# One fp32 block chain on one core: w3·w_out in the order of the tiles' conversion, output operands two units ahead, low parts on VectorE, output weights loaded further ahead

## The chip, the core and the metric

One core of a Trainium2 chip. The metric is the device time of the whole program in microseconds (us); less is better. Times shown are medians of several executions, and a profile is one further execution with the hardware profiler.

## What is computed

Attention with a bias of cumulative gates, then a feed-forward block with g = h - tanh(h), then a gated block whose two inner products are multiplied; all in fp32.

```python
x = attention(q, k, v, s)            # 2304 tokens x 512
h = x @ w_in; x = (h - tanh(h)) @ w_out
a = x @ w1;  b = x @ w2              # 2304 x 1024 each
h = a * b @ w3                       # 1024 x 1024
return h @ w_out2                    # 1024 x 512
```

## The kernel before

Every fp32 matrix is split into a high part, the value cast to the matmul's short fp32 type (ScalarE, line 64), and a low part, the rest (line 65: `lo`, on GpSimd if the caller names no other). A product is three matmuls: high*high, high*low, low*high (`mm3`, line 113).

There are three phases. The first, to about 425 us, is attention, mixed with half of the feed-forward block. The second (`ffn_rest`) is the other half; beside it `preparations` (line 654) brings the weights of the last block into shape: w1 and w2 into seven sums and differences for each of eight column groups (DRAM tensor `wg_d`), and w3 into `w3_d`, eight tiles f = 0 to 7 of 1 MB, high and low part. A tile is converted into a `park` buffer, of which there are two, and stored (line 683).

The third phase has two steps. First, w3 @ w_out2 is worked out (lines 820 to 837), so that the last two products become one. For each f the tile is loaded from `w3_d` into a `park` buffer (`w3b`, line 823), 24 matmuls make `w3o`, and ScalarE copies it to a ring tile `wf` (line 831). `weights` makes from each four of these one half h of the seven output weights (`wkA`, `wkS`), which line 817 stores to `wo_d`, 512 KB each; the first half's are made in this loop, the second's in the first seven units. In the loop also stand the loads of the weights S and A of units 0 and 1 (`load_unit`, behind tiles 2 and 4), and `need(0)`, which makes one operand of the first token block at each step.

Second, the two products with w1 and w2, the multiplication, and the product with the combined weight run over three blocks `sb` of 768 tokens, as seven-product schemes (Strassen-Winograd: T1 to T4 are sums and differences of the operand quarters B11 to B22, S1 to S4 those of the weights). A unit u is a block and a column group f, 24 in all. It has seven groups of six matmuls of 384 columns, in the order A11 (bank W), A12 (V), S2 (W), S4 (Y), S3 (W), then S1 of the next unit (Y, `first_y`), A22 (W). Between them ScalarE copies (s1, u2, s5) and VectorE adds (c11 from V, c12 from Y, c22 from W) take the partial sums out; Y has one bank, so the next unit's Y waits for c12, and A22 waits for c22. Two multiplications (lines 966 and 967, the second on GpSimd) give a quarter of the next product's operand.

The combined weight's product for block sb (`class Out`) is done in the units of block sb + 1: at f = 0 to 6 two bursts of 12 matmuls, `burst(f, 0)` behind A12 and `burst(f, 1)` behind S4. A burst needs `operand(f)`, made at the end of the unit before: for T1 to T4 two subtractions (tso, line 885), and for all two casts on ScalarE and two low parts on VectorE, into one of two ring buffers. It needs the weight `load(f)`, issued one unit ahead into four half buffers `wo`. At the last block nothing follows, and the seven products run as a tail of 24 matmuls each (lines 981 to 987).

At the change of block, `operands(sb + 1)` makes seven operands of the next block; in it GpSimd makes the low parts of B11, B21 and B22, and VectorE those of T1 to T4 (line 769).

DMAs are issued by SyncE's queue (SP) alone. A planner orders the instructions of each engine by a simulated timeline, and may move them ahead of their place in the program; on TensorE it keeps program order where `manual_schedule` has been entered, in the kernel before from line 841 on, so behind the w3 loop. An engine runs its queue in order.

Of the kernel before, what the change touches and what calls it, by code (L numbers as in the profile page):

```python
# [15 lines left out]
P = 128  # L16
# [3 lines left out]
DM = 512  # L20
# [17 lines left out]
def tile_kernel(ctx: ExitStack, tc: tile.TileContext, qk, v, s, w_in, w_out, w1, w2, w3t, w_o2, outT):  # L38
# [24 lines left out]
    def split(dst_hi, dst_lo, src, hi=None, lo=None):  # L63
        i = (hi or nc.scalar.copy)(dst_hi, src)  # L64
        (lo or nc.gpsimd.tensor_sub)(dst_lo, src, dst_hi.bitcast(F32))  # L65
        return i
# [584 lines left out]
    def load_w3(f, z):  # L651
        return load_raw(w3t[f, :, 4 * z:4 * z + 4].rearrange("p m c -> p (m c)"), f"w3_{f}_{z}", behind=pace[0])

    def preparations():

        for f in range(NG):
            a = plain(load_raw(w1[f], f"w1_{f}", behind=pace[0]), f"w1_{f}")
            yield
            b = plain(load_raw(w2[f], f"w2_{f}", behind=pace[0]), f"w2_{f}")
            a11, a12, a21, a22 = a[:, :2 * P], a[:, 2 * P:], b[:, :2 * P], b[:, 2 * P:]  # L660
            cs = b2.tile([P, 4, 2 * P], F32, tag="cs", name=f"cs{f}", bufs=1)
            for z, (x, y, fn) in enumerate(((a21, a22, nc.vector.tensor_add), (cs[:, 0], a11, nc.vector.tensor_sub),
                                            (a11, a21, nc.vector.tensor_sub), (a12, cs[:, 1], nc.vector.tensor_sub))):
                fn(cs[:, z], x, y)
            pk = wt.tile([P, 4, 2, 2 * P], F32R, tag="park", name=f"pka{f}", bufs=2)
            for z, x in ((0, a[:, :].rearrange("p (z c) -> p z c", z=2)), (2, a22.unsqueeze(1))):
                n = x.shape[1]
                split(pk[:, z:z + n, 0], pk[:, z:z + n, 1], x, lo=nc.vector.tensor_sub)
            nc.sync.dma_start(wg_d[f, :, 4:], pk[:, :3].bitcast(F32))
            pk = wt.tile([P, 4, 2, 2 * P], F32R, tag="park", name=f"pks{f}", bufs=2)  # L670
            split(pk[:, :, 0], pk[:, :, 1], cs, lo=nc.vector.tensor_sub)
            nc.sync.dma_start(wg_d[f, :, :4], pk.bitcast(F32))
            yield
        for f in range(NG):
            if f == NG // 2:
                for m in range(NG):
                    convert(load_raw(w_o2[m], f"wo2_{m}", behind=pace[0]), f"wo2_{m}", wo2[m], lo=nc.vector.tensor_sub)
                    yield
            pk = wt.tile([P, 2, 2, DM], F32R, tag="park", name=f"w3p{f}", bufs=2)
            for z in range(2):  # L680
                convert(load_w3(f, z), f"w3_{f}_{z}", pk[:, z], lo=nc.vector.tensor_sub)
                yield
            nc.sync.dma_start(w3_d[f], pk.bitcast(F32))

    with ExitStack() as bctx:
        b2 = bctx.enter_context(tc.tile_pool(name="b2", bufs=2, reuse_waits="tile"))
# [67 lines left out]
    def operands(sb):  # L754

        c0 = 2 * T * sb
        b11, b12, b21, b22 = (xy[:, c:c + 2, c0 + T * t:c0 + T * t + T] for c in (0, 2) for t in (0, 1))
        full = {"B11": b11, "B21": b21, "B22": b22}
        out = {}
        for o in OPS:  # L760
            if o in full:
                x = full[o]
            else:
                x = r3.tile([P, 2, T], F32, tag="ts", name=f"{o}_{sb}", bufs=2)
                full[o] = x
                a, b = {"T1": (b12, b11), "T2": (b22, full["T1"]), "T3": (b22, b12), "T4": (b21, full.get("T2"))}[o]
                nc.vector.tensor_sub(x, a, b)
            w = r3.tile([P, 2, 2, T], F32R, tag="tb", name=f"{o}hl_{sb}", bufs=8)
            split(w[:, 0], w[:, 1], x, lo=nc.vector.tensor_sub if o[0] == "T" else None)
            out[o] = w  # L770
            yield out

# [4 lines left out]
    def load_unit(u):  # L777
        if u >= len(units):
            return
        f = units[u][1]  # L780
        ws = r3.tile([P, 4, 2, 2 * P], F32R, tag="ws", name=f"S_{u}", bufs=2)
        nc.sync.dma_start(ws.bitcast(F32), wg_d[f, :, :4])
        wa = r3.tile([P, 3, 2, 2 * P], F32R, tag="wa", name=f"A_{u}", bufs=2)
        nc.sync.dma_start(wa.bitcast(F32), wg_d[f, :, 4:])
        wts[u] = {o: ws[:, n] if n < 4 else wa[:, n - 4] for o, n in WOP.items()}
# [13 lines left out]
    def ring(name):  # L799
        return r3.tile([P, 6, DM], F32, tag="ring", name=name, bufs=2)  # L800
# [17 lines left out]
            yield  # L818

    wf, made, last = [], [], {}  # L820
    for f in range(NG):
        w3 = wt.tile([P, 2, 2, DM], F32R, tag="park", name=f"w3b{f}", bufs=2)
        nc.sync.dma_start(w3.bitcast(F32), w3_d[f])
        if f in (2, 4):
            load_unit(f // 2 - 1)
        ps = ps3.tile([P, 512], F32, tag=f"o{f % 2}", name=f"w3o{f}")
        for m in range(NG):
            mm3(ps, w3[:, m // 4], P * (m % 4), wo2[m][:, 0, :], wo2[m][:, 1, :], m == 0, m == NG - 1)
        if f % 4 == 0:
            wf.append(ring(f"wf{f // 4}"))  # L830
        nc.scalar.copy(wf[-1][:, f % 4], ps)
        if f % 4 == 3:
            made.append(weights(f // 4, wf[-1]))
        if f >= NG // 2:
            for _ in range(2):
                next(made[0], None)
        need(0)

    lctx.close()
    l3 = ctx.enter_context(tc.tile_pool(name="l3", bufs=2, reuse_waits="tile"))  # L840
    ctx.enter_context(tc.manual_schedule(engines={mybir.EngineType.PE}))

    def temp(name, u, dt=F32):
        return l3.tile([P, T], dt, tag=name, name=f"{name}_{u}")
# [18 lines left out]
    class Out:  # L863
# [25 lines left out]

        def load(self, n):  # L890
            self.ws[n] = []
            for h in range(2):
                k = r3.tile([P, 2, 2, 2 * P], F32R, tag="wo", name=f"wo{n}_{h}_{self.sb}", bufs=4)
                after_pe(nc.sync.dma_start(k.bitcast(F32), wo_d[n, h]), last.get("pe"))
                self.ws[n].append(k)

# [30 lines left out]
    for u, (sb, f) in enumerate(units):  # L927
# [7 lines left out]
        last["pe"] = group(w, wu["A11"], b["B11"], True, False)  # L935
        if old and f < 6:
            old.load(f + 1)
        if f == NG - 1:
            new.load(0)
        s1 = temp("s1", u)  # L940
        nc.scalar.copy(s1, w[:, :T])
        vv = bank("V", f"V_{u}")
        group(vv, wu["A12"], b["B21"], True, True)
        c11 = temp("c11", u)
        nc.vector.tensor_add(c11, vv[:, :T], s1)
        if old and f < 7:
            old.burst(f, 0)
        group(w, wu["S2"], b["T2"], False, False)
        u2 = temp("u2", u)
# [2 lines left out]
        c12 = temp("c12", u)  # L952
        nc.vector.tensor_add(c12, y[:, :T], u2)
        if old and f < 7:
            old.burst(f, 1)
        group(w, wu["S3"], b["T3"], False, False)
        c22 = temp("c22", u)
        last["c22"] = nc.vector.tensor_add(c22, w[:, :T], s5)  # L958
        if nxt:
            y, s5 = first_y(u + 1)  # L960
        group(w, wu["A22"], b["T4"], False, True)
        if nxt and f == NG - 1:
            for _ in OPS[1:]:
# [3 lines left out]
        (nc.gpsimd if nxt else nc.vector).tensor_mul(new.b[d2][:, f // 2], c12, c22)  # L967
        if sb == 0:
            next(made[1], None)
        if old and f < 6:  # L970
            old.operand(f + 1)
        if f == 6:
            if u < len(units) - 2:
                got = operands(sb + 1)
# [4 lines left out]
            new.operand(0 if nxt else 1)  # L979
    last.clear()  # L980
    for n in range(7):
        if n < 6:
            new.load(n + 1)
        for j in range(2):
            new.burst(n, j)
        if n < 5:
            new.operand(n + 2)
# [39 lines left out]
```

## Time and profile before

| | us |
|---|---|
| runs, median (all three) | 954.67 (949.22, 954.67, 955.17) |
| profiled execution | 953.33 |
| its span, first to last instruction | 951.5 |
| TensorE matmuls busy | 921.0 |
| VectorE busy | 646.5 |
| ScalarE busy | 452.2 |
| GpSimd busy | 231.0 |

The profile names engines PE (TensorE's matmuls), PEld (its weight loads), DVE (VectorE), ACT (ScalarE), POOL (GpSimd) and SP (SyncE); "SPq" is an instruction by which SP issues a DMA. L65 is line 65. A tile's name has its buffer numbers left out: `w3b<-w_d` is the load of a w3 tile, `oY<-T1o,wo` a burst. Matmuls are pipelined: one's start-to-start distance is less than its duration. The granted clock is a share of TensorE's full 2.4 GHz; its other level is 1.2 GHz.

### The profile page before, as it was taken

To read this page: it belongs to the slowest core of one execution; us is meant where nothing else is said; L and a number is where in the kernel's file an instruction comes from. 1 tells how busy PE (TensorE), PEld (TensorE's weight loads), DVE (VectorE), ACT (ScalarE), POOL (GpSimd) and SP (SyncE) were. 2 spreads that over 40 slices of the span, in tenths; PEclk is the share of its full clock that TensorE was granted. 3 is DMA by queue.
4 is the path that set the end of the run, shared out by engine and by line. 5 is a ranking of instruction groups with operands and counts; after the bars stand their busy time and mean duration, and the time that the engine had idled before them with its cause. 6 is when DMAs were issued, how large, how long until landed. Compare 5 with 4: busy or idle time off the path is not lost.

```text
span 951.5 us, 16425 instructions
## 1 busy us (share of the span) xinstructions
PE 921.0 (97%) x6022; PEld 803.0 (84%) x6025; DVE 646.5 (68%) x1394; ACT 452.2 (48%) x1061; POOL 231.0 (24%) x219
## 2 busy tenths in 40 slices
PE   8889999899999999999999999998999999999998
PEld 4467778788888889998888888986899999999997
DVE  7677767687787866767999887673145546744654
ACT  4457877777777743324544343332124232433233
POOL 2245756556565410000000000020024111311100
PEclk9799999999999999999999999999999999999999
DMA  5555365435444523499788644668399767776746
GB/s 161 192 160 171 112 199 189 170 126 183 147 167 145 179 91 98 147 355 362 265 287 302 215 146 177 220 268 295 118 323 332 285 238 288 269 268 234 274 174 218
DMA packets 59648, 203.41 MB, mean 214 GB/s; under 512 B 6608, under 2 KB 21104, under 8 KB 53424
## 3 DMA queue, kind: packets, MB, share of 16 engines
q1 hardware_dynamic: 59568, 202.37, 61.2%
q8 instruction: 47, 0.77, 0.3%
q14 instruction: 33, 0.27, 0.1%
HBM read 153.95 MB, written 48.39 MB: 213 GB/s over the span
## 4 chain that ended last, share of the span: by engine, by line
PE 77%; DVE 9%; DMA 6%; issue 3%; ACT 3%; POOL 1%; SPq 1%; ACTq 0%; DVEq 0%; POOLq 0%
PE yb L117 10%; PE hb L117 10%; PE h L117 8%; PE W L849 8%; PE y L431 7%; PE oW L906 5%; PE w3o L117 4%; PE s_B L229 4%; PE Y L849 4%; PE pv L327 4%; PE oY L906 4%; PE pt_B L301 3%; DVE tso L885 2%; DMA cb<-cum_d 1%; PE V L849 1%
## 5 line engine op out<-in xcount | busy, mean ns | idle before, releaser
L117 PE MATMUL h<-xhl,win 128*128 128x256 f32 x864 | 121.2, 286 | 2.7 <-DVE xhl L65 2.2
L117 PEld LDWEIGHTS h<-xhl,win 128*128 128x128 f32 x864 | 106.2, 188 | 13.7 <-issue 3.9
L117 PE MATMUL hb<-x,win 128*128 128x512 f32 (+1 forms) x480 | 104.9, 367 | 0.0
L117 PEld LDWEIGHTS hb<-x,win 128*128 128x128 f32 x480 | 83.9, 188 | 15.0
L117 PE MATMUL yb<-ghb,wout 128*128 128x512 f32 (+1 forms) x320 | 95.6, 367 | 0.0
L206 POOL TENSOR_SCALAR pr<-cb,cq 128x384 f32<-128x384 f32 (+1 forms) x48 | 89.1, 1869 | 25.0 <-DMA cb<-cum_d 15.2
L431 PE MATMUL y<-gh,wout 128*128 128x256 f32 x576 | 85.5, 288 | 0.0
L290 ACT ACTIVATE pr<-pr,nm 128x128 f32<-128x128 f32 (+2 forms) x120 | 71.5, 598 | 18.6 <-DVE nm L268 18.4
L431 PEld LDWEIGHTS y<-gh,wout 128*128 128x128 f32 x576 | 72.8, 189 | 3.0 <-issue 2.0
L65 POOL TENSOR_TENSOR B11hl<-xy,B11hl 128x768 fp32r<-128x768 f32 x3 | 5.8, 1931 | 276.8 <-ACT B11hl L64 276.8
L117 PEld LDWEIGHTS yb<-ghb,wout 128*128 128x128 f32 x320 | 58.2, 188 | 9.9
L117 PE MATMUL yb<-glb,wout 128*128 128x512 f32 (+1 forms) x160 | 58.4, 367 | 0.0
L301 PE MATMUL pt_B<-ident,pr 96*128 96x96 f32 (+1 forms) x384 | 52.3, 260 | 1.9 <-DVE xy L364 1.0
L967 POOL TENSOR_TENSOR xy<-c,c 128x384 f32<-128x384 f32 x12 | 15.3, 1278 | 148.7 <-DVE c L958 148.7
L117 PE MATMUL w3o<-wo,w3b 128*128 128x512 f32 x192 | 46.0, 400 | 3.9 <-DMA w3b<-w_d 3.9
L268 DVE CUSTOM_DVE_ANT_0 pr<-s_B,pr 96x512 f32<-96x512 f32 (+1 forms) x72 | 44.2, 638 | 8.0 <-PE s_B L229 7.8
L431 PE MATMUL y<-gl,wout 128*128 128x256 f32 x288 | 45.4, 280 | 3.8 <-POOL gl L65 3.8
L117 PEld LDWEIGHTS w3o<-wo,w3b 128*128 128x128 f32 x192 | 36.9, 194 | 12.4 <-issue 4.6
L301 PEld LDWEIGHTS pt_B<-ident,pr 96*128 96x128 f32 (+1 forms) x384 | 41.9, 144 | 6.3 <-issue 3.4
L310 ACT COPY pf_B<-pt_B 128x512 f32<-128x512 f32 (+2 forms) x72 | 35.8, 499 | 22.7 <-PE pt_B L301 22.7
L463 DVE TENSOR_TENSOR th<-h,th 128x256 f32<-128x256 f32 x72 | 30.0, 417 | 22.5 <-ACT th L460 21.7
L460 ACT ACTIVATE th<-h 128x256 f32<-128x256 f32 x72 | 26.9, 374 | 35.3 <-PE h L117 35.3
(213 smaller groups left out, 2093.6 us busy)
## 6 DMA issues: line engine op xcount, KB each, us to landing
S<-wg_d SPq DMA_DIRECT2D x24, 1024.0 KB
wo<-wo_d SPq DMA_DIRECT2D x42, 512.0 KB
A<-wg_d SPq DMA_DIRECT2D x24, 768.0 KB
qk<-in_qk SPq DMA_DIRECT2D x16, 576.0 KB
raw_win<-in_w_in SPq DMA_DIRECT2D x16, 512.0 KB
raw_wout<-in_w_out SPq DMA_DIRECT2D x16, 512.0 KB
raw_w<-in_w SPq DMA_DIRECT2D x16, 512.0 KB
wg_d<-pks SPq DMA_DIRECT2D x8, 1024.0 KB
```

The lines of the kernel that those rows point to most:

```text
L117: i = nc.tensor.matmul(ps, a, b, start=first and n == 0, stop=last and n == 2, skip_group_check=skip)
L206: nc.gpsimd.tensor_scalar(out=t[:pw, e, :w], in0=p.cb[:pw, e, :w], scalar1=c, scalar2=0.0, op0=ALU.add, op1=ALU.min)
L229: latest[0] = nc.tensor.matmul(ps[e][:PW[i], o:o + k1 - k0], w[r, 0, CH0[i]:CH0[i] + PW[i]], x[r, 1, k0:k1], start=z == 0 and (not p.first ...
L268: least[0] = nc.vector.tensor_tensor_reduce(out=t[:pw, k0:k1], in0=ps[:pw, o:o + k1 - k0], in1=t[:pw, k0:k1], scale=-0.125, scalar=nm[:pw, ...
L290: last_exp[0] = nc.scalar.activation(t[:pw, :], t[:pw, :], AF.Exp, bias=m, scale=-1.0, accum_out=p.sums[:pw, e, c:c + 1])
L301: nc.tensor.transpose(pt[:, at:at + pw], p.pr[i][:pw, e, KC0[kj]:KC0[kj] + P], ident[:pw, :pw])
L310: (nc.vector.tensor_copy if j == "B2" and not p.first else nc.scalar.copy)(pf[:, :at], pt[:, :at])
L327: nc.tensor.matmul(p.pv[D * e:D * e + D, c:p.nq], p.vs[:, e, kj], pf[:, beg:end], start=z == 0, stop=z == len(todo) - 1, skip_group_check= ...
L431: nc.tensor.matmul(o, wout[f][:, z, P * c:P * c + P], x, start=f == 0 and n == 0 and c % 2 == 0, stop=f == F1 - 1 and n == 2, skip_group_c ...
L463: nc.vector.tensor_sub(t, hh, t)
L849: i = nc.tensor.matmul(ps[:, :T], w[:, x, P * j:P * j + P], b[:, y, j], start=first and j == n == 0, stop=stop and j == 1 and n == 2, skip ...
L906: nc.tensor.matmul(ps[:, :T], w[:, a, q % 2, P * j:P * j + P], x[:, b, q], start=o in ("B11", "B21", "T1") and q == z == 0, stop=o in ("T4 ...
```

## The change

1. The w3 loop takes the tiles in the order 6, 7, 4, 5, 0, 1, 2, 3. Tiles 6 and 7, the last that are converted, stay in their two `park` buffers, and their stores and loads fall away; the other six are loaded as before, each when a buffer comes free. TensorE keeps program order from the loop on. The loads of units 0 and 1 stand in steps 3 and 5 of the loop in place of 2 and 4 (counted from 0).
2. `operand(f + 2)` takes the place of `operand(f + 1)` at a unit's end; `operand(1)` is made in unit f = 0 behind s1, and the burst (0, 0) moves behind S4 and c12, beside (0, 1).
3. The low parts of B11, B21 and B22 are made by VectorE.
4. At the last block `load(0)` is issued in unit 6 and `load(1)` in unit 7; odd products load into the wide buffer `ws` of the unit weights, and loads in the tail are issued up to three products ahead.
5. In the last unit, `burst(0, 0)` stands ahead of A22, and the tail begins with `burst(0, 1)`.

```diff
--- before.py
+++ after.py
@@ -651,6 +651,8 @@
     def load_w3(f, z):
         return load_raw(w3t[f, :, 4 * z:4 * z + 4].rearrange("p m c -> p (m c)"), f"w3_{f}_{z}", behind=pace[0])
 
+    W3ORDER, kept = (6, 7, 4, 5, 0, 1, 2, 3), {}
+
     def preparations():
 
         for f in range(NG):
@@ -680,7 +682,10 @@
             for z in range(2):
                 convert(load_w3(f, z), f"w3_{f}_{z}", pk[:, z], lo=nc.vector.tensor_sub)
                 yield
-            nc.sync.dma_start(w3_d[f], pk.bitcast(F32))
+            if f in W3ORDER[:2]:
+                kept[f] = pk
+            else:
+                nc.sync.dma_start(w3_d[f], pk.bitcast(F32))
 
     with ExitStack() as bctx:
         b2 = bctx.enter_context(tc.tile_pool(name="b2", bufs=2, reuse_waits="tile"))
@@ -766,7 +771,7 @@
                 a, b = {"T1": (b12, b11), "T2": (b22, full["T1"]), "T3": (b22, b12), "T4": (b21, full.get("T2"))}[o]
                 nc.vector.tensor_sub(x, a, b)
             w = r3.tile([P, 2, 2, T], F32R, tag="tb", name=f"{o}hl_{sb}", bufs=8)
-            split(w[:, 0], w[:, 1], x, lo=nc.vector.tensor_sub if o[0] == "T" else None)
+            split(w[:, 0], w[:, 1], x, lo=nc.vector.tensor_sub)
             out[o] = w
             yield out
 
@@ -818,27 +823,34 @@
             yield
 
     wf, made, last = [], [], {}
-    for f in range(NG):
-        w3 = wt.tile([P, 2, 2, DM], F32R, tag="park", name=f"w3b{f}", bufs=2)
-        nc.sync.dma_start(w3.bitcast(F32), w3_d[f])
-        if f in (2, 4):
-            load_unit(f // 2 - 1)
-        ps = ps3.tile([P, 512], F32, tag=f"o{f % 2}", name=f"w3o{f}")
+    w3b = dict(kept)
+
+    def fetch_w3(f):
+        if f not in w3b:
+            w3b[f] = wt.tile([P, 2, 2, DM], F32R, tag="park", name=f"w3b{f}", bufs=2)
+            nc.sync.dma_start(w3b[f].bitcast(F32), w3_d[f])
+        return w3b[f]
+
+    ctx.enter_context(tc.manual_schedule(engines={mybir.EngineType.PE}))
+    for n, f in enumerate(W3ORDER):
+        w3 = fetch_w3(f)
+        if n in (3, 5):
+            load_unit(n // 2 - 1)
+        ps = ps3.tile([P, 512], F32, tag=f"o{n % 2}", name=f"w3o{f}")
         for m in range(NG):
             mm3(ps, w3[:, m // 4], P * (m % 4), wo2[m][:, 0, :], wo2[m][:, 1, :], m == 0, m == NG - 1)
-        if f % 4 == 0:
-            wf.append(ring(f"wf{f // 4}"))
+        if n % 4 == 0:
+            wf.append(ring(f"wf{n // 4}"))
         nc.scalar.copy(wf[-1][:, f % 4], ps)
-        if f % 4 == 3:
+        if n % 4 == 3:
             made.append(weights(f // 4, wf[-1]))
-        if f >= NG // 2:
+        if n >= NG // 2:
             for _ in range(2):
                 next(made[0], None)
         need(0)
 
     lctx.close()
     l3 = ctx.enter_context(tc.tile_pool(name="l3", bufs=2, reuse_waits="tile"))
-    ctx.enter_context(tc.manual_schedule(engines={mybir.EngineType.PE}))
 
     def temp(name, u, dt=F32):
         return l3.tile([P, T], dt, tag=name, name=f"{name}_{u}")
@@ -889,8 +901,14 @@
 
         def load(self, n):
             self.ws[n] = []
+            wide = None
+            if self.sb == NSB - 1 and n % 2:
+                wide = r3.tile([P, 4, 2, 2 * P], F32R, tag="ws", name=f"wo{n}_{self.sb}", bufs=2)
             for h in range(2):
-                k = r3.tile([P, 2, 2, 2 * P], F32R, tag="wo", name=f"wo{n}_{h}_{self.sb}", bufs=4)
+                if wide is None:
+                    k = r3.tile([P, 2, 2, 2 * P], F32R, tag="wo", name=f"wo{n}_{h}_{self.sb}", bufs=4)
+                else:
+                    k = wide[:, 2 * h:2 * h + 2]
                 after_pe(nc.sync.dma_start(k.bitcast(F32), wo_d[n, h]), last.get("pe"))
                 self.ws[n].append(k)
 
@@ -935,15 +953,20 @@
         last["pe"] = group(w, wu["A11"], b["B11"], True, False)
         if old and f < 6:
             old.load(f + 1)
-        if f == NG - 1:
+        if f == NG - 1 - (sb == NSB - 1):
             new.load(0)
+        elif f == NG - 1:
+            new.load(1)
         s1 = temp("s1", u)
-        nc.scalar.copy(s1, w[:, :T])
+        last["s1"] = nc.scalar.copy(s1, w[:, :T])
+        if old and f == 0:
+            last["s5"] = last["s1"]
+            old.operand(1)
         vv = bank("V", f"V_{u}")
         group(vv, wu["A12"], b["B21"], True, True)
         c11 = temp("c11", u)
         nc.vector.tensor_add(c11, vv[:, :T], s1)
-        if old and f < 7:
+        if old and 0 < f < 7:
             old.burst(f, 0)
         group(w, wu["S2"], b["T2"], False, False)
         u2 = temp("u2", u)
@@ -952,12 +975,16 @@
         c12 = temp("c12", u)
         nc.vector.tensor_add(c12, y[:, :T], u2)
         if old and f < 7:
+            if f == 0:
+                old.burst(f, 0)
             old.burst(f, 1)
         group(w, wu["S3"], b["T3"], False, False)
         c22 = temp("c22", u)
         last["c22"] = nc.vector.tensor_add(c22, w[:, :T], s5)
         if nxt:
             y, s5 = first_y(u + 1)
+        else:
+            new.burst(0, 0)
         group(w, wu["A22"], b["T4"], False, True)
         if nxt and f == NG - 1:
             for _ in OPS[1:]:
@@ -967,8 +994,8 @@
         (nc.gpsimd if nxt else nc.vector).tensor_mul(new.b[d2][:, f // 2], c12, c22)
         if sb == 0:
             next(made[1], None)
-        if old and f < 6:
-            old.operand(f + 1)
+        if old and f < 5:
+            old.operand(f + 2)
         if f == 6:
             if u < len(units) - 2:
                 got = operands(sb + 1)
@@ -979,9 +1006,11 @@
             new.operand(0 if nxt else 1)
     last.clear()
     for n in range(7):
-        if n < 6:
-            new.load(n + 1)
-        for j in range(2):
+        if n == 0:
+            new.load(2)
+        if n < 4:
+            new.load(n + 3)
+        for j in range(n == 0, 2):
             new.burst(n, j)
         if n < 5:
             new.operand(n + 2)
```

## Rows read from the trace of the kernel before

**Rows 1.** The page, part 1: busy time, share of the span, instructions.

```profile
PE 921.0 (97%) x6022; PEld 803.0 (84%) x6025; DVE 646.5 (68%) x1394; ACT 452.2 (48%) x1061; POOL 231.0 (24%) x219
```

**Rows 2.** Waits of PE, 620 to 951 us: us in total, times, longest.

```profile
PE w3o L117 <- DMA w3b<-w_d: 3.9, 1, 3.9
PE W L849 <- ACT s L941: 1.4, 1, 1.4
PE Y L849 <- DVE c L953: 1.3, 2, 0.8
PE oW L906 <- DVE B11o L65: 0.9, 2, 0.5
PE oW L906 <- DMA wo<-wo_d: 0.8, 1, 0.8
PE W L849 <- DVE c L958: 0.7, 1, 0.7
PE oY L906 <- DVE T1o L65: 0.4, 2, 0.2
```

**Rows 3.** Chain that ended last, 650 to 690 us: start, us, what.

```profile
655.20 9.38 DMA w3b<-w_d
...
664.72 12.77 PE w3o L117 x48
...
680.25 1.04 PE Y L849 x6
```

**Rows 4.** Windows: length, busy us by engine, clock, DMA share, GB/s.

```profile
596.00:624.00 28.00, 28.00 (x215) 26.89 (x214) 14.52 (x30) 7.98 (x19) 0.00 (x0) 1.00 0.58 203
634.00:636.00 2.00, 2.00 (x11) 1.73 (x10) 1.97 (x2) 0.00 (x0) 1.14 (x1) 1.00 0.46 188
664.70:670.10 5.40, 5.38 (x17) 4.28 (x18) 0.00 (x0) 0.00 (x0) 0.00 (x0) 0.68 0.64 267
731.40:741.10 9.70, 8.40 (x48) 7.76 (x46) 9.67 (x10) 5.10 (x8) 5.80 (x3) 1.00 0.99 380
```

**Rows 5.** Timeline of SP, 622 to 631 us: start, us, engine, instruction.

```profile
622.00 0.32 SPq L782 DMA_DIRECT2D S<-wg_d  x1
...
623.31 0.71 SPq L784 DMA_DIRECT2D A<-wg_d  x1
630.26 0.32 SPq L823 DMA_DIRECT2D w3b<-w_d  x1
```

**Rows 6.** Timeline of PE, 624 to 765 us; in brackets the idle time before.

```profile
624.63 11.04 PE L117 MATMUL w3o<-wo,w3b 128*128 128x512 f32 x48
635.51 1.20 PE L849 MATMUL Y<-T1hl,S 128*128 128x384 f32 x6
...
732.28 1.21 PE L849 MATMUL W<-T3hl,S 128*128 128x384 f32 x6
734.34 1.32 PE L849 MATMUL Y<-T1hl,S 128*128 128x384 f32 x6 [0.85 <-DVE c L953]
...
762.25 0.34 PE L906 MATMUL oY<-T1o,wo 128*128 128x384 f32 x1
...
764.80 1.20 PE L849 MATMUL W<-T2hl,S 128*128 128x384 f32 x6
```

**Rows 7.** Timeline of DVE, 728 to 742 us.

```profile
731.40 2.42 DVE L65 TENSOR_TENSOR T2hl<-T,T2hl 128x768 fp32r<-128x768 f32 x1 [0.37 <-ACT T2hl L64]
...
734.67 1.65 DVE L65 TENSOR_TENSOR T3hl<-T,T3hl 128x768 fp32r<-128x768 f32 x1
736.35 1.66 DVE L767 TENSOR_TENSOR T<-xy,T 128x768 f32<-128x768 f32 x1
...
740.14 0.95 DVE L65 TENSOR_TENSOR T4hl<-T,T4hl 128x768 fp32r<-128x768 f32 x1
```

**Rows 8.** Timeline of POOL, 728 to 742 us.

```profile
731.16 1.84 POOL L65 TENSOR_TENSOR B21hl<-xy,B21hl 128x768 fp32r<-128x768 f32 x1
```

**Rows 9.** Stores of output weights, 620 to 670 us: durations, first and last start.

```profile
L817 SPq DMA_DIRECT2D wo_d<-wkS x4: 319/319/319, 652.4 to 657.7; - x4
```

## The prediction

> **What bounds the kernel now.** I read the page first: TensorE (PE) is busy 97% of the span [rows 1], and in the last 28 us of the second phase it is busy 28.00 of 28.00 [rows 4]. What VectorE, the DMA queues and HBM do there is hidden, so nothing that the change removes ahead of 624 us can pay. I then asked whom PE waits for from 620 us on [rows 2], and the timelines around each wait. Every wait of PE from there on is in that list: ten lines (seven stand there; those for T2o, T3o and T4o read like T1o's, 0.4 us in 2 times), 10.6 us in total. The rest is matmuls at a fixed rate: a group of six takes 1.04 us [rows 3], a tile of w3 5.44 us (48 matmuls for two tiles, 635.51 - 624.63 = 10.88) [rows 6]. The change leaves the number of matmuls alone. So it is worth the waits that it takes away, less those that it makes.
>
> A wait costs more than its idle time, since the first matmuls behind it are slower. The 12 matmuls of the T1o burst begin at 762.25 and the next group at 764.80: 2.55 us where two groups would be 2.08, so 0.47 for an idle time of 0.2 [rows 2, 3, 6]. I add the difference, 0.27, to every wait.
>
> **Operands two units ahead.** T1o, T2o, T3o and T4o are made at the end of a unit for a burst some 3 us later, and the burst waits for VectorE's low part. With a unit more of lead (11.4 us: seven groups and two bursts of 2.08) they are there. Eight waits (four lines, 2 times each) by 0.47: **-3.8**. Their instructions are the same, only earlier; the ring of two buffers is free, since operand f+2 takes the buffer of operand f, whose bursts stand ahead of S3 in the same unit.
>
> **First burst of a block behind S4 and Y.** B11o gets 2.08 us more (S2 and S4, a group each), and its two waits were 0.9 in all [rows 2], 1.45 with the addition: **-1.45**. B21o's making moves from the end of unit 0 to its start: two casts on ScalarE and two low parts on VectorE, queued between s1 and u2, and between c11 and c12. Those behind them, u2 and c12, are wanted only behind two bursts, 4.16 us later, so that is free.
>
> **Low parts of B11, B21, B22 on VectorE.** At the change of block VectorE takes over three subtractions of 0.95 us (the duration of T4hl's) [rows 7], 2.85 in all, twice. Against it: T2hl's took 2.42 beside GpSimd's B21hl (731.16 for 1.84) [rows 7, 8], 1.47 more than T4hl's. T3hl's low part (1.65) and the subtraction for T4 (1.66) behind it are 0.7 above it each [rows 7]. That adds up to 2.9, so VectorE's load there stays about the same. The Trainium skill, SBUF — State Buffer, Terms, says that VectorE and GpSimd take turns at one port pair, and the loser "fully blocks" for the whole instruction; the row agrees, T2hl's end at 733.82 being 0.82 behind the end of B21hl's at 733.00. By that rule the whole 2.9 goes away with GpSimd's work; by the rows alone it could be anything from none to all.
>
> What it does to PE: Y of the next block waited for c12 behind T2hl's: from W's S3 group at 732.28 to Y at 734.34 it is 2.06 where 1.04 is the rate, 1.02 lost; two such waits, 1.3 idle and 1.8 with the addition [rows 2, 6]. c12 can still stand behind one subtraction of 0.95, no longer behind one of 2.42. Bounds: all 1.8 comes back, or, if GpSimd's share was not the cause, 2.85 more a time is added. I take the half: **-0.9**.
>
> **The end.** The last unit has no next Y, so c22 holds up A22: 0.65 idle, 0.9 with the addition [rows 2]; the first output burst, 2.08 us, now stands between: **-0.9**. B21o's last half still needs A22's product, a cast and a low part, some 2.7 us; burst (0,1) and half of (1,0), 3.1 us, cover it, narrowly. The output weights, two products deep before, come up to four deep, in the freed wide buffers: the wait for wo, 0.8, goes: **-1.05**.
>
> **w3*w_out.** Nothing of the two stores and two loads less pays: they were under a full PE [rows 4]. Two things change.
> First, before, PE filled the time from 635.51 to 638.6 with Y, W and V of unit 0. Then those units' copies stood on ScalarE behind the last wf copy, and S2 waited 1.44 for s1. In program order Y, W, V come behind the last tile: their 3.12 us are paid there instead (no difference), and V covers s1's copy: **-1.7**.
> Second, without that filler the third tile (f=4) is wanted at 635.51. Its load is issued when the first tile's buffer is free, at 630.26 as before, behind four loads of S and A (622.00 to 623.31, 3.67 MB) [rows 5]. By the windows these five moved 188 GB/s in 634 to 636 us [rows 4], 0.38 MB, some 1.0 us at the 380 GB/s of a stretch in which the DMA engines are busy throughout (731.4 to 741.1): last byte at about 635.0. The completion comes some time behind it. Bounds: no wait, or to 636.0, 0.5 idle; I take the upper end: **+0.5**.
> The Trainium skill, DMA: Bandwidth & Descriptors, Anatomy of one DMA, gives 2 us and 1/436e9 s for a byte: 4.4 us, landing at 634.7. By it this term were 0 and the time 0.5 less. The chain shows that a load behind others takes longer, 9.38 for the one issued at 655.20 [rows 3].
>
> That one, the seventh tile's, is the largest wait: 3.92 idle, and behind it the granted clock is 0.68 of full over 5.4 us (664.7 to 670.1) [rows 4], its two levels, 1.2 and 2.4 GHz, mixed; the 48 matmuls from 664.72 took 12.6 where 10.88 is the rate. Together 3.9 + 0.2 + 1.7 = 5.8 us. Its cause is left: the stores of the wo parts, 512 KB each (four of S from 652.4 to 657.7) [rows 9], are made behind the fourth tile now as then, and the load of the seventh is issued behind the fifth. I take it as unchanged: **0**, with -5.8 to 0 as bounds.
>
> **Sum.** -3.8 - 1.45 - 0.9 - 0.9 - 1.05 - 1.7 + 0.5 = -9.3; 0.3 back for new small waits, at B21o's last half or at the change of block: -9.0. The profiled execution took 953.33 (1.8 around its span): 953.33 - 9.0 = **944.3**. The three runs are 949.22, 954.67 and 955.17, so the profile lies 1.3 below the median, and the lowest run lies about one late seventh tile below the others. I predict **944.5**.
>
> **Rivals.**
> *The seventh tile lands in time.* The removed transfers and new order shift what meets in the queue; the 6 us between the three runs speak for such luck, the unchanged stores against. Of its 5.8 some 0.3 of idle time may be left: 944.5 - 5.5 = 939.
> *VectorE becomes the bound at the change of block.* For it: VectorE is busy there for 9.67 of 9.70 us from 731.4 [rows 4], with c12 and c22 in its queue. Against it: it is free of GpSimd. The gain of 0.9 falls away and 2.85 are added a time: 944.3 + 0.9 + 5.7 = 951.
> *PE in order, without filler, makes it slower than before.* A tile that is late now stops PE, as the seventh did, at 5.6 us a tile with the clock's share. The S and A loads (1.8 MB a unit, 4.8 us at 380 GB/s) now stand at the fourth and sixth tile. If the planner issues them there, rather than at 622 us, a w3 load meets one and is 4.8 us later; the margin is under 1 us (5.44 between the tiles, 630.26 to about 635 for a load). One late tile leaves a gain of 3.4; from the second on, the kernel is slower: three give 944.3 + 16.8 = 961, four 967. Against it: SP issued S and A as soon as their buffers came free, when nothing else was ready.
> *The lead does nothing.* If operand f+2 must wait for its ring buffer until the unit's end, the 3.8 stays: 948.
>
> **How the numbers follow.** Forecast 0.50 (its own range 941 to 948, with the clock's chance and half of each uncertain term); seventh tile in time 0.23; VectorE the bound 0.12; lead without effect 0.05; late tiles 0.07; the rest 0.03. A measurement of this kernel tells about 1% from no change, here 9.5 us: faster is under 945.1. Of the forecast about 0.6 lies there, 0.30, and all of the seventh tile's 0.23: 0.53. Slower, over 964.2, takes four late tiles, half of that rival's chance and a little for what I have not seen: 0.05. Same: 0.42. The range goes from 938.5, the early tile with 0.5 to spare, to 950.5, VectorE the bound at nearly full price; beyond it lie late tiles and a share of the others.
>
> **What would show it.** Right: no wait of oY and oW for T1o to T4o or B11o; none for s1 at the first S2; A22 of the last unit straight behind a burst; none for wo. The third w3 tile waits under 1 us; the seventh waits 3 to 4 us with the clock falling behind it. Wrong: S and A issued behind 635 us, more than one idle stretch in w3o, the clock down more than once, or a wait of Y at the change of block that is longer than 1 us.

## The result, and the profile after

| | us | ratio to before, 95% interval |
|---|---|---|
| before, median of 5 runs (946.91 to 955.17) | 949.97 | |
| changed, median of 5 runs (941.84 to 945.42) | 942.70 | 0.992 (0.989 to 0.994) |
| changed, measured again beside three experiments, 7 runs (939.29 to 946.42) | 943.89 | 0.993 (0.990 to 0.996) |

The kernel became some 7 us, 0.8%, faster. That is inside the range and 1.8 us from the time forecast. Two more runs brought the median of the kernel before from 954.67 to 949.97, and the gain is 7.3 us in place of the 10.2 from there to 944.5: by the prediction's bound of 1% this is "same", which the chances had at 0.42 against 0.53 for faster.

Who PE waits for in the changed kernel, 615 to 951 us (in total, times, longest). In place of the ten lines of before [rows 2] there are three:

```profile
PE w3o L117 <- DMA w3b<-w_d: 5.2, 4, 2.8
PE W L861 <- ACT s L961: 0.8, 2, 0.4
PE W L861 <- DMA A<-wg_d: 0.3, 1, 0.3
```

No output burst waits any more, neither does Y for c12, nor A22 for c22 [rows 2, 6]. One line has grown: w3b, 3.9 in one wait before, is 5.2 in four. The wait for s1 at the first S2 is gone; that line now stands for two new ones, for s1 at the two changes of block. The wait for the unit weight A is new as well.

The spans, 951.5 and 940.9, differ by 10.6, more than the medians. I cut all profiles at three places of TensorE's timeline: the first `hb` (end of the first phase), the first `w3o`, and the first S2 of unit 0.

| profile | first phase | second | w3 loop and Y, W, V | units and tail |
|---|---|---|---|---|
| before | 426.4 | 198.2 | 54.3 | 269.2 |
| changed | 424.2 | 198.2 | 52.9 | 262.3 |
| changed, again (x12) | 425.6 | 198.2 | 51.6 | 263.4 |

Of the 10.6, 2.3 lie ahead of the loop (its first matmul starts at 624.63 and 622.35), in the first phase, which the change does not touch: TensorE's order of instructions is the same in both up to the loop. Over the fourteen profiles of this study it took 420.5 to 431.2 us; the rows of the tile `hb` (duration min/median/max, then first and last start) of the two outermost, x6 below:

```profile
L117 PE MATMUL hb<-x,win x480: 278/389/395, 420.5 to 614.3; 128*128 128x512 f32 x128, 128*128 128x256 f32 x32
```

and x3 below:

```profile
L117 PE MATMUL hb<-x,win x480: 278/389/395, 431.2 to 625.0; 128*128 128x512 f32 x128, 128*128 128x256 f32 x32
```

So one profile against another says nothing on 2 us of the total; the stages do. 1.4 lie in the loop and 6.8 in the units and the tail.

**The loop after.** Timeline of PE (start, us, instruction, in brackets the idle time before):

```profile
622.35 11.04 PE L117 MATMUL w3o<-wo,w3p 128*128 128x512 f32 x48
633.82 11.14 PE L117 MATMUL w3o<-wo,w3b 128*128 128x512 f32 x48 [0.42 <-DMA w3b<-w_d]
646.50 11.12 PE L117 MATMUL w3o<-wo,w3b 128*128 128x512 f32 x48 [1.54 <-DMA w3b<-w_d]
660.48 5.72 PE L117 MATMUL w3o<-wo,w3b 128*128 128x512 f32 x24 [2.85 <-DMA w3b<-w_d]
666.55 5.72 PE L117 MATMUL w3o<-wo,w3b 128*128 128x512 f32 x24 [0.35 <-DMA w3b<-w_d]
672.11 1.20 PE L861 MATMUL Y<-T1hl,S 128*128 128x384 f32 x6
```

The two kept tiles (`w3p`) run without a wait. The third waits 0.42 (forecast 0.5), the fifth 1.54, the seventh 2.85, the eighth 0.35. The chain has the loads of the third, the fifth and the eighth, from issue to landing: 5.65, 6.82 and 8.75, where a tile takes 5.44.

```profile
628.03 5.65 DMA w3b<-w_d
...
639.55 6.82 DMA w3b<-w_d
...
657.66 8.75 DMA w3b<-w_d
```

**The change of block after.** PE:

```profile
732.49 1.20 PE L861 MATMUL W<-B11hl,A 128*128 128x384 f32 x6
733.53 1.21 PE L861 MATMUL V<-B21hl,A 128*128 128x384 f32 x6
735.14 1.32 PE L861 MATMUL W<-T2hl,S 128*128 128x384 f32 x6 [0.40 <-ACT s L961]
736.30 1.20 PE L861 MATMUL Y<-B22hl,S 128*128 128x384 f32 x6
737.34 4.32 PE L924 MATMUL oW<-B11o,wo 128*128 128x384 f32 x24
...
744.62 1.20 PE L861 MATMUL W<-B11hl,A 128*128 128x384 f32 x6
```

What S2 waited for, on ScalarE, VectorE and GpSimd:

```profile
731.80 1.57 ACT L64 CAST B11o<-xy 128x768 fp32r<-128x768 f32 x2
733.88 0.83 ACT L64 CAST T4hl<-T 128x768 fp32r<-128x768 f32 x1 [0.50 <-DVE T L772]
734.61 0.47 ACT L961 COPY s<-W 128x384 f32<-128x384 f32 x1
```

```profile
732.18 1.66 DVE L772 TENSOR_TENSOR T<-xy,T 128x768 f32<-128x768 f32 x1
```

```profile
731.36 1.66 POOL L994 TENSOR_TENSOR B22o<-c,c 128x384 f32<-128x384 f32 x1 [7.31 <-DVE c L983]
```

T4hl's cast waits 0.50 for VectorE's subtraction, and s1's copy stands behind the cast. That subtraction takes 1.66 beside GpSimd's multiplication, as it did before [rows 7].

But the copy is no later than it was. S2 adds to bank W, which the copy reads first. In the kernel before the copy starts 2.25 behind A11's first matmul (738.79 - 736.54), in the changed kernel 2.12 (734.61 - 732.49). What differs is the first burst: before it stood between A12 and S2, and S2 was wanted only at 741.45.

```profile
736.54 1.20 PE L849 MATMUL W<-B11hl,A 128*128 128x384 f32 x6
...
739.41 2.20 PE L906 MATMUL oW<-B11o,wo 128*128 128x384 f32 x11 [0.45 <-DVE B11o L65]
741.45 1.20 PE L849 MATMUL W<-T2hl,S 128*128 128x384 f32 x6
```

```profile
738.79 0.47 ACT L941 COPY s<-W 128x384 f32<-128x384 f32 x1
```

**The end after.** A burst stands between S3 and A22, and nothing waits:

```profile
906.21 1.20 PE L861 MATMUL W<-T3hl,S 128*128 128x384 f32 x6
907.25 2.24 PE L924 MATMUL oW<-B11o,wo 128*128 128x384 f32 x12
909.33 1.20 PE L861 MATMUL W<-T4hl,A 128*128 128x384 f32 x6
```

### The profile page after: what moved, and what is told of

It is laid out like the page before. It is cut to its first block, busy times and chain, and to the rows that moved or that the text cites. A ratio compares the mean times of both kernels' runs of the same rounds, so it can differ in the third digit from the quotient of the medians.

```text
span 940.9 us, 16373 instructions
## 1 busy us (share of the span) xinstructions
PE 914.4 (97%) x6022; PEld 800.3 (85%) x6025; DVE 641.4 (68%) x1403; ACT 452.6 (48%) x1061; POOL 211.7 (22%) x210
## 4 chain that ended last, share of the span: by engine, by line
PE 81%; DMA 7%; DVE 5%; ACT 3%; issue 2%; POOL 1%; SPq 1%; ACTq 0%; DVEq 0%; POOLq 0%
PE hb L117 10%; PE yb L117 10%; PE h L117 9%; PE W L861 9%; PE y L431 9%; PE oW L924 5%; PE Y L861 5%; PE s_B L229 4%; PE pv L327 4%; PE oY L924 4%; PE pt_B L301 3%; PE w3o L117 2%; DMA w3b<-w_d 2%; PE V L861 2%; DMA cb<-cum_d 2%
## 5 line engine op out<-in xcount | busy, mean ns | idle before, releaser
L872 ACT COPY s<-Y 128x384 f32<-128x384 f32 x24 | 11.6, 482 | 63.0 <-PE Y L861 60.5
L431 PEld LDWEIGHTS y<-gl,wout 128*128 128x128 f32 x288 | 38.3, 188 | 3.8 <-POOL gl L65 3.1
L64 ACT CAST ghb<-thb 128x512 fp32r<-128x512 f32 (+1 forms) x40 | 23.2, 579 | 35.2 <-DVE thb L725 34.5
```

The source lines that it names most:

```text
L431: nc.tensor.matmul(o, wout[f][:, z, P * c:P * c + P], x, start=f == 0 and n == 0 and c % 2 == 0, stop=f == F1 - 1 and n == 2, skip_group_c ...
```

## The experiments

My theory was the prediction's: the gain is the sum of waits taken off PE, each worth its idle time and 0.27. Against it stood: a wait only moves to another engine; the order of the loop does more (or less) than its waits say; the late w3 tiles come from the stores in the queue, or from HBM. Four kernels undo a part each, four change one suspected cause or two, and four settle what was left. Each was timed against the kernel before; their stages:

| kernel | median, us | ratio, 95% interval | loop | units and tail |
|---|---|---|---|---|
| x1 loop as before | 943.61 | 0.991 (0.988 to 0.993) | 53.1 | 262.2 |
| x2 no lead, first burst back | 947.69 | 0.996 (0.993 to 0.999) | 51.7 | 266.2 |
| x3 low parts on GpSimd | 946.65 | 0.994 (0.991 to 0.997) | 52.7 | 263.9 |
| x4 end as before | 946.55 | 0.994 (0.992 to 0.996) | 55.8 | 265.7 |
| x5 held stores | 940.49 | 0.988 (0.986 to 0.990) | 50.1 | 262.4 |
| x6 before, held stores | 949.02 | 0.995 (0.993 to 0.998) | 49.8 | 270.0 |
| x7 multiplication on VectorE | 941.25 | 0.991 (0.987 to 0.994) | 53.7 | 261.4 |
| x8 x5 and x7 | 939.42 | 0.988 (0.986 to 0.990) | 48.9 | 262.6 |
| x9 w3 tiles in halves | 936.10 | 0.985 (0.982 to 0.989) | 47.4 | 262.0 |
| x10 x5, x7 and x9 | 935.82 | 0.985 (0.982 to 0.988) | 46.7 | 261.7 |
| x11 first burst back | 943.54 | 0.992 (0.989 to 0.994) | 56.5 | 263.6 |
| x12 changed, again | 943.89 | 0.993 (0.990 to 0.996) | 51.6 | 263.4 |

The intervals are some 3 us to either side, so differences of 1 or 2 us between two kernels are read from the stages.

### x1: the w3 loop as it was

```diff
-    w3b = dict(kept)
...
-    for n, f in enumerate(W3ORDER):
-        w3 = fetch_w3(f)
+    for f in range(NG):
+        w3 = wt.tile([P, 2, 2, DM], F32R, tag="park", name=f"w3b{f}", bufs=2)
+        nc.sync.dma_start(w3.bitcast(F32), w3_d[f])
```

> The changed kernel with the w3 loop as it was: tiles 0 to 7, all stored and loaded, TensorE in program order only behind the loop. If the waits simply add up, the loop's gain is the 1.4 us by which the two traces differ from the start of w3o to the first S2 of unit 0 (54.3 to 52.9): 1 to 2 us slower than the changed kernel, one wait of PE for w3b with a lower clock behind it, Y, W and V of unit 0 between the second and third tile, and a wait of about 1.4 for s1. If the loop's order is what keeps the clock up, 3 to 6 us slower, since a late tile then costs half a tile at the lower clock again. If the order of the tiles is worth nothing, within 0.5 us.

943.61, the same as the changed kernel (942.70 and 943.89). The loop took 53.1, with the wait of 1.4 for s1 and a seventh tile that is 3.49 late, and TensorE's clock stays up behind it:

```profile
662.85 5.73 PE L117 MATMUL w3o<-wo,w3b 128*128 128x512 f32 x24 [3.49 <-DMA w3b<-w_d]
669.03 5.72 PE L117 MATMUL w3o<-wo,w3b 128*128 128x512 f32 x24 [0.45 <-DMA w3b<-w_d]
```

So the order of the loop and the two kept tiles together are worth nothing that can be measured here. The loops of the seven profiles that have the new order and the stores in their old place took 51.6 to 56.5; those of the two with the old order, 53.1 and 54.3. What the old order lost at s1 the new one loses at the fifth tile and others, which have no filler any more.

### x2: no lead

This undoes both parts of point 2 of the change, the lead and the moved burst.

```diff
-        if old and f == 0:
-            last["s5"] = last["s1"]
-            old.operand(1)
...
-        if old and 0 < f < 7:
+        if old and f < 7:
...
-        if old and f < 5:
-            old.operand(f + 2)
+        if old and f < 6:
+            old.operand(f + 1)
```

> The changed kernel with operands made one unit ahead again, and the first burst of a block behind A12 again. If each of these waits was on the path: the eight waits of T1o to T4o (0.47 each) and the two of B11o come back, 4.5 to 5.3 us slower. If the lead only moves the wait to another engine, so that ScalarE's s1 copy at the change of block (0.7 twice in the changed kernel) is its price, 3 to 4 us slower, with the waits for s1 gone.

Units and tail are 3.8 longer than the changed kernel's, and the eight waits are back, each 0.2 idle:

```profile
PE oY L924 <- DVE T1o L65: 0.4, 2, 0.2
...
PE oW L924 <- DVE T2o L65: 0.4, 2, 0.2
PE oW L924 <- DVE T3o L65: 0.4, 2, 0.2
PE oW L924 <- DVE T4o L65: 0.4, 2, 0.2
```

From unit 9 to unit 15 it takes 70.7 us as before (70.6), where the changed kernel takes 68.6; from 17 to 23 it is the same. So the lead alone is worth 2.0 a block, 4.0 in all. The two waits for B11o are not listed any more:

```profile
735.04 2.69 PE L924 MATMUL oW<-B11o,wo 128*128 128x384 f32 x12
```

It is 2.53 us to the next group (737.57) in place of 2.83 before, where two groups at the rate take 2.08: 0.45 of the 0.75 is left, in pauses too short for the list. Unit 8 takes 11.89 (732.96 to 744.85), less than the 12.13 of the changed kernel. The waits for s1 are gone, but the copy is as late as in the changed kernel, 2.13 behind A11 (735.09 - 732.96):

```profile
735.09 0.47 ACT L961 COPY s<-W 128x384 f32<-128x384 f32 x1
```

What took the wait away is the burst, which stands between A12 and S2 again. So the wait is the price of the moved burst. It is not the price of the lead: x11 keeps that and has no wait for s1 either.

### x3: the low parts of B11, B21, B22 on GpSimd

```diff
-            split(w[:, 0], w[:, 1], x, lo=nc.vector.tensor_sub)
+            split(w[:, 0], w[:, 1], x, lo=nc.vector.tensor_sub if o[0] == "T" else None)
```

> The changed kernel with the low parts of B11, B21 and B22 on GpSimd again. If GpSimd's work holds up VectorE: T2hl's low part takes 2.4 us again beside it, Y of the next block waits for c12, 1 to 2 us slower in all. If VectorE's load at the change of block is the same either way (2.85 added, 2.9 of stretching gone), within 0.5 us of the changed kernel.

Units and tail are 1.5 longer, 1.2 of it in units 7, 8, 15 and 16. Y waits for c12 again, T2hl's low part takes 2.41 again, and there is the wait for s1 beside it:

```profile
PE Y L861 <- DVE c L976: 1.3, 2, 0.8
PE W L861 <- ACT s L961: 1.1, 2, 0.5
```

```profile
735.10 2.41 DVE L65 TENSOR_TENSOR T2hl<-T,T2hl 128x768 fp32r<-128x768 f32 x1 [0.37 <-ACT T2hl L64]
```

The wait for c12 came from GpSimd's work: without it the low parts of all seven operands fit on VectorE. No burst waits for B11o here, and this kernel still has the moved burst. B11o's low parts are as late as in the kernel before, ending 3.68 behind A11's first matmul in both (743.91 - 740.23, and 740.22 - 736.54; before's row stands first):

```profile
738.41 1.81 DVE L65 TENSOR_TENSOR B11o<-xy,B11o 128x768 fp32r<-128x768 f32 x2
```

```profile
742.10 1.81 DVE L65 TENSOR_TENSOR B11o<-xy,B11o 128x768 fp32r<-128x768 f32 x2
```

So with GpSimd at work it is the moved burst that hides B11o.

### x4: the end as before

```diff
-        if f == NG - 1 - (sb == NSB - 1):
+        if f == NG - 1:
             new.load(0)
-        elif f == NG - 1:
-            new.load(1)
...
-        else:
-            new.burst(0, 0)
```

> The changed kernel with the end as it was: the first output burst behind A22, weights two products deep, no wide buffers. If both waits come back (c22 before A22 0.9, wo in the T2o burst 1.0): 1.7 to 2.0 us slower. If the deeper loading is not needed once load(0) finds its buffers free, only c22's: 0.9 us.

From unit 23's first group to the last matmul it takes 37.8, as before (38.0), in place of 35.9: 1.9 for the end. The other 1.4 of the stage lie in units 0 to 7, where every profile has waits for S and A in another amount. c22's wait is back:

```profile
PE W L861 <- DVE c L975: 0.6, 1, 0.6
```

That is some 0.9 of the 1.9. The wait for wo is not listed again; the rest is spread over the last products, where B22o's 24 matmuls take 4.46 (928.39 to 932.85) in place of 4.16. What holds them was not followed up.

### x5 and x6: stores held until the seventh tile

The same edit on the changed kernel and on the kernel before: all products of the first half are made in step 6, and their stores wait for the first matmuls of that step.

```diff
-            mm3(ps, w3[:, m // 4], ...)
+            i = mm3(ps, w3[:, m // 4], ...)
+            if n == 6 and not m:
+                last["w3"] = i
...
-        if n >= NG // 2:
-            for _ in range(2):
-                next(made[0], None)
+        if n == 6:
+            for _ in made[0]:
+                pass
+            last.pop("w3")
```

> The changed kernel with the stores of the first half's output weights held until the first matmuls of the seventh w3 tile (in program step 6), so that no w3 load has a store ahead of it or beside it. If the stores make the late tiles late: the waits for the seventh and eighth tile (2.85 and 0.35 idle) fall to under 0.5 together, the loop is 3 us shorter; the fifth tile's 1.5 stays if it has another cause. If slow reads of HBM make them late, stores or not, a wait of 1 us or more stays at the seventh tile and the time moves by less than 1.5 us.

> The kernel before with the stores held in the same way and nothing else changed. If the stores are the cause, the wait of 3.9 for the seventh tile and the lower clock behind it go: 3 to 6 us faster than the kernel before, and the spread of its runs (946.9 to 955.2) shrinks to some 3 us. If slow reads are the cause, the spread stays and the median moves by less than 2 us.

The loops are 50.1 and 49.8 us long: x5's is 1.5 to 2.8 shorter than in the two profiles of the changed kernel, x6's 4.5 shorter than before. The kernel before is 0.995 of itself with this edit alone (0.993 to 0.998), 3 us; its runs still spread over 940.9 to 952.2, so that part of x6's expectation did not come true: the spread has the first phase's 10 us in it. PE in x6:

```profile
632.64 27.37 PE L117 MATMUL w3o<-wo,w3b 128*128 128x512 f32 x120
661.28 5.68 PE L117 MATMUL w3o<-wo,w3b 128*128 128x512 f32 x24 [1.26 <-DMA w3b<-w_d]
```

Tiles three to seven run as one stretch. The wait has moved to the eighth, whose load now meets the stores: the stores make a tile late, whichever they meet. In x5 the eighth waits 1.25, and the fifth still waits 0.90 with no store near it, so they are one cause and not the only one.

### x7 and x8: the multiplication of unit 7 on VectorE

```diff
-        (nc.gpsimd if nxt else nc.vector).tensor_mul(
+        (nc.gpsimd if nxt and f < 7 else nc.vector).tensor_mul(
```

> The changed kernel with the second multiplication of unit 7 of a block (B22 = c12 * c22) on VectorE in place of GpSimd. If GpSimd stretches VectorE's subtraction for T4 (1.66 us beside it, 0.95 alone), and so delays T4hl's cast and s1's copy behind it on ScalarE, the two waits of S2 for s1 (0.68 each with the slower matmuls) fall to 0.3 or less: 0.5 to 1.2 us faster. If ScalarE's casts of B11o are what s1 stands behind, they stay as they are and the time is the same within 0.5 us.

> Held stores and the multiplication on VectorE together, on the changed kernel. If both causes are right, 3 to 4 us faster than the changed kernel, some 939 us. If only one is, that one's share.

Units and tail took 0.9 less than in the changed kernel, 0.7 of it in units 8 and 16, and no wait for s1 is listed. VectorE's subtraction takes 0.95 where it took 1.66:

```profile
730.25 0.95 DVE L772 TENSOR_TENSOR T<-xy,T 128x768 f32<-128x768 f32 x1
```

Units 8 and 16 are 11.8 long in place of 12.1; 11.4 is the rate, so half of the loss is left. In the medians of x7 (941.25) and x8 (939.42, beside x5's 940.49) this can't be told from noise. x8 comes out at its 939, and its profile has both gains, the loop at 48.9 and units 8 and 16 at 11.8; but only the loop's shows in the median.

### x9 and x10: w3 tiles in halves

```diff
-            w3b[f] = wt.tile([P, 2, 2, DM], F32R, tag="park", name=f"w3b{f}", bufs=2)
-            nc.sync.dma_start(w3b[f].bitcast(F32), w3_d[f])
+            w3b[f] = kept[W3ORDER[W3ORDER.index(f) % 2]]
+            for z in range(2):
+                nc.sync.dma_start(w3b[f][:, z].bitcast(F32), w3_d[f, :, z])
```

> The changed kernel with each w3 tile loaded as two halves of 512 KB into the two park buffers, so that the first half is issued when 12 of the buffer's 24 matmuls are done, 2.7 us earlier, and gets some 8 us in place of 5.4. The stores stay where they are. If the waits of PE in the loop are a load's own time against 5.44 us a tile, they fall from 5.2 to under 1.5 us in total. If they come from what stands in the queue ahead of the load (S and A, the stores), the seventh tile's stays over 1.5 us, and the loop gains 2 us or less.

> Halves, held stores and the multiplication of unit 7 on VectorE together, on the changed kernel. From the traces of these three: the loop near its 43.5 us of matmuls plus 3.1 for Y, W and V (46.7 to 47.5 from w3o to the first S2, against 52.9), and 0.9 less in the units: 6 to 7 us faster than the changed kernel, 935 to 937. If the loads are bound by what HBM gives, the loop stays over 48.5.

x9 is the clearest step of the study: 936.10 beside 943.89 for the changed kernel measured with it. In its stage it is less: the loop takes 47.4, 4.2 to 5.5 shorter than in the two profiles of the changed kernel. 180 matmuls of the loop run without a wait, stores and all:

```profile
622.43 41.22 PE L117 MATMUL w3o<-wo,w3p 128*128 128x512 f32 x180
663.85 3.01 PE L117 MATMUL w3o<-wo,w3p 128*128 128x512 f32 x12 [0.20 <-DMA w3p<-w_d]
```

By the chain the last half, beside the stores, took 7.34 us from issue to landing, more than the 5.44 that a whole tile has:

```profile
656.46 7.34 DMA w3p<-w_d
```

So the waits were a load's time against 5.44 us, whatever lengthened it: with some 8 us (5.44 + 2.72) all but 0.20 of them is gone. x10 has the loop at 46.7 us, its matmuls alone, and only one wait behind 610 us, 0.5 for S. It is the fastest by its median, 935.82, within noise of x9's.

### x11: the first burst back

```diff
-        if old and 0 < f < 7:
+        if old and f < 7:
...
+        if old and f == 0:
+            old.operand(1)
         if old and f < 5:
             old.operand(f + 2)
```

> The changed kernel with the first burst of a block behind A12 again and B21o made at the end of unit 0, everything else kept (operands two units ahead from unit 1 on, low parts on VectorE). By the prediction, which gave the moved burst 1.45, the two waits for B11o come back and the two units 8 and 16 are 0.7 longer each. By what the kernel without the lead showed (unit 8 took 11.89 there, 12.13 in the changed kernel), B11o is in time anyway once GpSimd is out of the way, and units 8 and 16 are 0.2 shorter each.

Unit 8 took 12.3, unit 16 11.9, against 12.1 in the changed kernel. Neither has a listed wait for B11o, though in unit 16 its burst takes 0.42 longer than the rate; unit 8 has a wait of 0.47 for the weight `wo`. The waits for s1 are gone here too. B21o, made later, costs 0.5 in units 9 and 17 (0.2 idle each, 11.9 in place of 11.4). Against the changed kernel the moved burst takes off the 0.42 and puts on s1's 0.69: by itself it is worth nothing.

### x12: the changed kernel again

> The changed kernel again, on the same chip as the three beside it, for comparison: some 942 us, the loop 52 to 54 us from w3o to the first S2, units 8 and 16 at 12.1.

943.89, the loop at 51.6, units 8 and 16 at 12.1.

## Why the prediction was right, and where it was not

| term | forecast | measured |
|---|---|---|
| operands two ahead | -3.8 | -4.0: 2.0 less from unit 9 to 15 and from 17 to 23 |
| first burst moved | -1.45 | B11o's wait gone, s1's (0.69 twice) in its place: units 8 and 16 0.06 and 0.04 shorter |
| low parts on VectorE, c12 | -0.9 | -1.0 (units 7 and 15), -1.2 with units 8 and 16 (x3) |
| the end | -0.9 - 1.05 | -2.1 (38.0 to 35.9), -1.9 (x4) |
| new small waits | +0.3 | some +0.4, weights of the first block's units; s1's stand above |
| s1 at the first S2; third tile | -1.7 + 0.5 | about 0: 51.6 to 56.5 against 53.1 and 54.3 |
| seventh tile | 0 | 5.8 to 3.1 in these two profiles; in the seven profiles of the new order it idles 0 to 3.24, and in x4 and x11, where that is little, the eighth idles 2.5 |

**Right.** Where PE is the bound and runs at a fixed rate, the sum of its waits is a good price. 0.27 for the slow matmuls behind a wait held: 0.40 idle for s1 cost 735.14 - 733.53 - 1.04 = 0.57 at the first matmul and 0.12 behind it, 0.69. For units and tail the sum was -3.8 - 1.45 - 0.9 - 1.95 + 0.3 = -7.8; they became 6.8 shorter, and what is missing lies in the main at the change of block.

**Missed: what the moved burst had covered.** The step moved the first burst from between A12 and S2, and asked whether u2 and c12 would be late, but not what the burst had hidden at its old place. That was s1's copy: it is as late before, in x2 and in the changed kernel (2.25, 2.13 and 2.12 behind A11), and S2 waits for it only where the burst no longer stands ahead (the changed kernel, x3), not in x2 and x11. So the burst's 1.45 was paid back as 0.69 twice. What makes the copy late stands ahead of it on ScalarE, B11o's two casts and T4hl's, and T4hl's waits for a VectorE subtraction that GpSimd's multiplication stretches. The Trainium skill, SBUF — State Buffer, Terms (the shared port pair), agrees once more: the subtraction ended 0.82 behind the multiplication's end (733.84 against 733.02), and without it took 0.95 (x7). The multiplication was left on GpSimd, and I had not counted it; without it half of the 0.69 goes (x7).

**Two edits for one wait: B11o.** The moved burst does what the step said: in x3, where B11o's low parts are as late as before, it hides them whole. But freeing VectorE of GpSimd takes 0.3 of the 0.75 a time without any move (x2, x11), so with both edits in, the burst's own part is the smaller, 0.42 to 0.45 a time.

**Wrong: the loop.** The forecast priced two waits of one profile and took the rest of the loop as it was. Without Y, W and V as filler the fifth tile is in the open too. Its load took 6.82 where the bound was "about 5": I had taken one load's time from one profile as the rule, and a margin of under 1 us as enough, in the very rival that named it. That rival, PE in order and without filler, was half right: four tiles were late, at 0.35 to 2.85 each, but its price of 5.6 a tile supposed the lower clock behind each, and S and A were issued early, as its "against" said. "More than one idle stretch in w3o" stood among the signs of being wrong, and it came; the clock that was to fall behind the seventh stayed at 1.00. The stores as the cause of the seventh tile's wait were named rightly (x6). The prediction's 4.4 us by the Trainium skill, DMA: Bandwidth & Descriptors, Anatomy of one DMA, is a fit for DMAs that GpSimd issues; those of SP's loads that the chain shows took 5.65 to 8.75.

**Wrong: the base.** The sum was made against one profile, 953.33, which lay 3.4 above the median of five runs. I took the spread of the three runs for the seventh tile's luck; holding the stores does not shrink it (x6), and the first phase alone varies by 10 us. Nothing of the change touched that, but it decided between faster and same. That the time came within 1.8 us is in part luck: the base was 4.7 too high, the gain 2.9 too large, and the two errors cancel in the main.

## What to carry to other kernels

Where the matmul engine runs at a fixed rate, list its waits and price an edit by those that it removes, plus a quarter microsecond each. Before moving work that fills the engine, look at what it hides at its old place: here a copy that had been late all along. A double buffer that is refilled only when the whole tile has been read leaves a load one tile's time; refilling each half as it is read (x9: some 8 us for each half) took 4.2 to 5.5 us off the loop. And place an edit in its stage before comparing totals: here an untouched stage varied by more than the change was worth.

## What the runs showed of the hardware

An idle stretch of PE in the loop did not cost the clock by its length alone. Windows of the 5.5 us behind a late tile (length, busy us by engine, granted clock, DMA share, GB/s) in x1, the changed kernel, x4 (its eighth tile) and x7, with 3.49, 2.85, 2.56 and 3.24 us idle ahead:

```profile
662.80:668.30 5.50, 5.45 (x24) 4.43 (x24) 0.00 (x0) 0.00 (x0) 0.00 (x0) 1.00 0.62 261
```

```profile
660.40:665.90 5.50, 5.42 (x24) 4.43 (x24) 0.00 (x0) 0.00 (x0) 0.00 (x0) 1.00 0.52 219
```

```profile
665.80:671.30 5.50, 5.43 (x18) 4.38 (x19) 0.00 (x0) 0.00 (x0) 0.00 (x0) 0.71 0.00 0
```

```profile
656.30:661.80 5.50, 5.45 (x13) 4.32 (x14) 0.00 (x0) 0.00 (x0) 0.00 (x0) 0.50 0.69 287
```

```profile
656.35 13.84 PE L117 MATMUL w3o<-wo,w3b 128*128 128x512 f32 x48 [3.24 <-DMA w3b<-w_d]
```

After 3.49 us the clock stayed at full, after 2.56 it fell (0.71, its levels of 2.4 and 1.2 GHz mixed), and after 3.24 the whole stretch ran at 1.2 GHz, 13 matmuls started in place of 24. x7's 48 matmuls took 13.84 us there, where 48 take 11.04 at the full clock. So a late tile costs its idle time, or up to 2.8 us more, and a single profile does not tell which it will be. Why, these runs don't show.

What makes a w3 load take 5.65 or 6.82 us where few stores are near stays open. The third's stands behind S and A. Beside the fifth's stands one store, issued 2.0 behind it (641.55), but the same store stands there in x12, where the fifth tile does not wait, and in x5, without it, the fifth waits 0.90. That it has to do with HBM was not shown.
